# Fifteen small loads on ScalarE's queue, and a wait for them, behind the copy of wq's product

## The chip, the cores and the metric

The kernel runs on one core of a Trainium2 chip. The metric is the device time of one execution in microseconds (us). The chip's engines run side by side and synchronise by semaphores: TensorE (matrix products), VectorE, ScalarE and GpSimd (elementwise work), and SyncE (SP), which only issues transfers. Sixteen DMA engines move the data. SP's loads go through one queue of these (queue 1 in the profile), ScalarE's through another (queue 10).

## The reference

One decode step for two rows x of 1024 numbers: attention over a cache, and a small MLP mixer, mixed by a gate.

```python
# x (2,1,1024); caches (2, 4 heads, 32768, 128); wq (1024,4096); wo (4096,1024); w3 (1024,3584); w4 (3584,1024)
g = sigmoid((x * gate_w).sum(-1, keepdims=True))
q = (x @ wq) -> (2, 32 heads, 1, 128)          # 8 query heads share one head of the cache
p = softmax(q @ k^T * 128 ** -0.5)             # over 32768 positions
a = (p @ v) @ wo
x1 = x + hs                                     # hs: shifts along a sequence of length 1 leave zeros
b = x1 + gelu(layernorm(x1) @ w3) @ w4
out = g * a + (1 - g) * b
```

With a sequence of length 1 all four shifts give zeros, so w1 and w2 are not read. All is float32.

## The kernel before

**Tiles.** Everything large passes through a ring of two buffers, `load0` and `load1` (in the code `ring[j]` or `flat[j]`), of 128 rows by 64 KB each, 8.4 MB. One load fills one buffer: 128 rows, each one packet of up to 64 KB. wq comes in two loads, w3 in two (56 KB a row), each of the eight pairs of batch and head (a "head" below) in two of K and two of V, w4 in two in the middle, wo in three and four small ones into `tail` at the end.

**The order.** All of these loads are issued by SP, written out in order in `load` (L218): each waits for a mark that the buffer is free again, then issues. The marks that matter at the start: w3's two loads wait for wq's products of that buffer (`q0`, `q1`), K of head 0 for w3's products (`h0`, `h1`), V of head 0 in the first buffer for the first half of head 0's products with K (`k0`), in the second buffer for VectorE's word `k1_free`, when all of these products are done. ScalarE issues one load, xg (x and the gate's weights), at the very start (L244).

**The start of the program on the engines.** TensorE multiplies x with wq (`project`, L358) into two banks, sc0 and sc1. VectorE copies sc0 and ScalarE sc1 (L407, L409) into `row`. VectorE rearranges them (L415), TensorE turns them (L421), and VectorE writes the result as q (`q_pad`, `q_cur`). TensorE then multiplies the normalised x with w3 (L358 again) into sc2 and sc3, which VectorE and ScalarE copy (L444, L446); VectorE rearranges (L451), TensorE turns (L459), and VectorE and ScalarE compute the gelu (L463 to L475). Behind L459 TensorE enters the loop over heads (`turn`): products with K (L494), maxima, softmax, transposes (L511), products with V (L520). The loop runs four heads, the products with w4 (L373, 512 columns each), four heads and the products with wo that fit the ring.

A `Line` is an engine with its own semaphore: `mark` has an instruction add one to it, `after` makes the engine wait for marks or for a semaphore's count. A load adds 16 to its semaphore when it has landed.

Of the kernel before, what the change touches and what calls it, by code (L numbers as in the profile page):

```python
# [73 lines left out]
def kernel(  # L74
# [52 lines left out]
    nc = tc.nc  # L127
    scale = DH ** -0.5

    def new(name, *shape, parts=P):  # L130
        return nc.alloc_sbuf_tensor(name, [parts, *shape], F32).ap()

    def bank(name):
        return nc.alloc_psum_tensor(name, [P, 512], F32).ap()
# [45 lines left out]
    f = new("f", REP)  # L180
    so_far = new("so_far", D // 2)
    out_sb = new("out_sb", 2, CHUNK)

    sc = [bank(f"sc{i}") for i in range(NI)]
    tr = [bank(f"tr{i}") for i in range(2)]
# [8 lines left out]
    def sem(name):  # L194
        cleared.append(nc.alloc_semaphore(name))
        return cleared[-1]

    stored = nc.alloc_semaphore("stored")
    pe, dve, act, pool = (Line(e, sem(n)) for e, n in (
        (nc.tensor, "pe"), (nc.vector, "dve"), (nc.scalar, "act"), (nc.gpsimd, "pool")))  # L200
# [2 lines left out]
    landed = [sem(f"landed{i}") for i in range(2)]  # L203
    w_in = [*landed, sem("w_in2")]
    got_x = sem("got_x")
    issued = sem("issued")
    copied = sem("copied")
    middle = slice(BASE, BASE + 2 * ROWS)
# [198 lines left out]
    d_q = dve.mark(nc.vector.tensor_copy(row[:, 0], sc[0]))  # L407
    act.after(done)
    a_q = act.mark(nc.scalar.copy(row[:, 1], sc[1]))  # L409

    twice = p.rearrange("p i t w q -> p (i t w q)")[:, :REP * P * 2].rearrange(
        "p (h w i q) -> p h w i q", h=REP, w=PART, i=2)
# [34 lines left out]
    n = KF // G  # L447
# [234 lines left out]
```

## Time and profile before

| | |
|---|---|
| median of 2 runs | 773.11 us (773.02 to 773.20) |
| profiled execution | 773.22 us, span 771.7 us |
| transferred | 331.48 MB in 6647 packets, 430 GB/s over the span |
| busy: TensorE / VectorE / ScalarE | 437.2 / 94.4 / 60.7 us |
| TensorE's mean granted clock | 0.77 |

The span runs from the first to the last instruction. Times in the timeline are microseconds from its start: start, time taken, engine, line, operation, the tile written and the tiles read, sizes, count, and in brackets the idle time before it with what ended it. An engine's name with a q (SPq, ACTq) is its sequencer, which waits and issues transfers. A row of the DMA view is a queue with its packets, megabytes and the share of 16 engines' time that they took in the stretch asked for; issues are listed with the microseconds from issue to landing. A row of a table by stretches gives for each engine the busy time and count, then TensorE's granted clock, the DMA share and GB/s.

### The profile page before, as it was taken

To read this page: it belongs to the slowest core of one execution; us is meant where nothing else is said; L and a number is where in the kernel's file an instruction comes from. 1 tells how busy PE (TensorE), PEld (TensorE's weight loads), DVE (VectorE), ACT (ScalarE), POOL (GpSimd) and SP (SyncE) were. 2 spreads that over 40 slices of the span, in tenths; PEclk is the share of its full clock that TensorE was granted. 3 is DMA by queue.
4 is the path that set the end of the run, shared out by engine and by line. 5 is a ranking of instruction groups with operands and counts; after the bars stand their busy time and mean duration, and the time that the engine had idled before them with its cause. 6 is when DMAs were issued, how large, how long until landed. Compare 5 with 4: busy or idle time off the path is not lost. (4 is left out here: it accounts for less than half of the span.)

```text
span 771.7 us, 7007 instructions
## 1 busy us (share of the span) xinstructions
PE 437.2 (57%) x3116; PEld 191.4 (25%) x3116; DVE 94.4 (12%) x269; ACT 60.7 (8%) x144; POOL 4.4 (1%) x13
## 2 busy tenths in 40 slices
PE   0574747465656464546465456564645474556577
PEld 0231413232323232223221123231322232223232
DVE  1110202100210021002100002100210021002110
ACT  0000002000200020002100002000200020002000
POOL 2000000000000000000000000000000000000000
PEclk9977666866886778776876668767877777768769
DMA  9999999999999999999999999999999999999997
GB/s 381 435 436 436 435 436 435 436 432 435 435 435 435 435 428 435 428 435 435 427 437 437 432 435 435 435 435 435 435 435 435 435 435 431 435 435 435 421 427 321
DMA packets 6647, 331.48 MB, mean 430 GB/s; under 512 B 872, under 2 KB 1008, under 8 KB 1264
## 3 DMA queue, kind: packets, MB, share of 16 engines
q1 hardware_dynamic: 6496, 331.36, 99.4%
q8 instruction: 6, 0.10, 0.0%
q10 hardware_dynamic: 144, 0.01, 0.0%
q14 instruction: 1, 0.01, 0.0%
HBM read 331.36 MB, written 0.01 MB: 429 GB/s over the span
## 5 line engine op out<-in xcount | busy, mean ns | idle before, releaser
L494 PE MATMUL sc<-load,q_cur 128*32 128x512 f32 x1024 | 148.5, 740 | 128.9 <-PEq L53 128.9
L520 PE MATMUL pv<-load,pt 128*32 128x512 f32 x1024 | 135.7, 690 | 88.1 <-PEq L53 88.1
L494 PEld LDWEIGHTS sc<-load,q_cur 128*32 128x32 f32 x1024 | 53.7, 132 | 218.0 <-issue 213.2
L520 PEld LDWEIGHTS pv<-load,pt 128*32 128x32 f32 x1024 | 40.8, 125 | 173.0 <-issue 173.0
L511 PE MATMUL sc<-wide,p 128*128 128x128 f32 x256 | 43.7, 343 | 22.8 <-PEq L53 22.8
L577 DVE TENSOR_REDUCE mx<-sc 128x1 f32<-128x512 f32 x32 | 21.4, 689 | 286.9 <-PE sc L494 286.9
L561 ACT ACT_TABLE_LOAD x8 | 10.3, 1283 | 487.4 <-ACTq L53 487.4
L511 PEld LDWEIGHTS sc<-wide,p 128*128 128x128 f32 x256 | 39.5, 182 | 30.0 <-issue 30.0
L373 PE MATMUL acc<-load,w_pad 128*32 128x512 f32 x224 | 32.9, 730 | 18.9 <-PEq L53 18.9
L594 DVE COPY pt<-sc 64x256 f32<-64x256 f32 x64 | 25.9, 415 | 79.2 <-PE sc L511 78.4
L567 ACT COPY pt<-sc 64x256 f32<-64x256 f32 x64 | 23.5, 368 | 83.1 <-PE sc L511 80.6
L599 DVE COPY pv_sb<-pv 128x512 f32<-128x512 f32 x16 | 10.3, 687 | 147.9 <-PE tr L526 147.9
L530 PE MATMUL tr<-sel,pv_sb 128*128 128x8 f32 x128 | 19.7, 290 | 11.8 <-PEq L53 11.8
L530 PEld LDWEIGHTS tr<-sel,pv_sb 128*128 128x128 f32 x128 | 19.2, 237 | 12.3 <-issue 12.3
L358 PE MATMUL sc<-load,x_pad 128*32 128x512 f32 x128 | 18.0, 724 | 7.3 <-PEq L53 7.3
L561 ACT ACTIVATE p<-sc,bias 128x512 f32<-128x512 f32 x32 | 21.6, 686 | 0.1
L358 PE MATMUL sc<-load,xn_pad 128*32 128x384 f32 (+1 forms) x128 | 14.2, 600 | 10.3 <-PEq L53 10.3
L373 PEld LDWEIGHTS acc<-load,w_pad 128*32 128x32 f32 x224 | 9.1, 131 | 41.0 <-issue 41.0
L343 PE MATMUL tr<-xg_sb,perm 128*128 128x16 f32 x4 | 1.0, 372 | 23.0 <-DMA xg_sb<-xg 23.0
L590 DVE COPY p<-p 128x256 f32<-128x256 f32 x32 | 9.4, 294 | 26.7 <-ACT p L561 26.7
L358 PEld LDWEIGHTS sc<-load,xn_pad 128*32 128x32 f32 x128 | 4.5, 120 | 20.5 <-issue 20.5
L358 PEld LDWEIGHTS sc<-load,x_pad 128*32 128x32 f32 x128 | 4.7, 131 | 19.7 <-issue 19.7
(89 smaller groups left out, 91.9 us busy)
## 6 DMA issues: line engine op xcount, KB each, us to landing
load<-w SPq DMA_DIRECT2D x4, 7168.0 KB, 25.3
load<-wo SPq DMA_DIRECT2D x1, 7168.0 KB, 27.3
load<-wo SPq DMA_DIRECT2D x1, 4608.0 KB, 17.9
load<-wo SPq DMA_DIRECT2D x1, 2560.0 KB, 23.7
tail<-wo SPq DMA_DIRECT2D x1, 1024.0 KB, 25.7
tail<-wo SPq DMA_DIRECT2D x1, 640.0 KB, 26.8
load<-kt SPq DMA_DIRECT2D x16, 29.8
load<-vt SPq DMA_DIRECT2D x16, 29.2
```

What stands on the lines that cost most here:

```text
L358: last = nc.tensor.matmul(b[C * g:C * g + C, :hi - lo], pad[:, k], t[:, o + lo:o + hi], start=(k == 0), stop=(k == KD - 1))
L373: inst = nc.tensor.matmul(acc[lo:lo + C], lhsT, rows[:, g * (D // 2):(g + 1) * (D // 2)], start=False, stop=last, skip_group_check=True)
L494: last = nc.tensor.matmul(sc[i][C * g:C * g + C], q_cur[:, w, s], ring[j][:, w, o:o + 512], start=(s == 0 and w == 0), stop=(s == 1 and w ...
L511: last = nc.tensor.transpose(sc[k][:, t * P:(t + 1) * P], pair.rearrange("p w q -> p (w q)"), ident)
L520: last = nc.tensor.matmul(pv[C * g:C * g + C], pt[j][w][:, lo:lo + C], ring[j][:, w, o:o + G * DH], start=(j == 0 and w == 0 and t == 0), ...
L530: last = nc.tensor.matmul(tr[1][:, w * REP:(w + 1) * REP], pv_sb[:, s, w].rearrange("p i q -> p (i q)"), sel[:, s], start=(s == 0), stop=( ...
L561: nc.scalar.activation(p[:, i, :, :PART], sc[i].rearrange("p (t q w) -> p t w q", t=NT, w=PART), AF.Exp, bias=bias, scale=scale, accum_out ...
L567: nc.scalar.copy(*halves(1, j, c)).then_inc(pt_in, 1)
L577: last = [nc.vector.reduce_max(out=mx[:, k:k + 1], in_=sc[k], axis=AX.X) for k in ((1, 2) if i == 2 else (i,))][-1]
L590: nc.vector.tensor_copy(p[:, i, :, PART], p[:, i, :, 0]).then_inc(to_pe, 1)
L594: nc.vector.tensor_copy(*halves(0, j, c)).then_inc(pt_in, 1)
L599: last = nc.vector.tensor_copy(pv_sb[:, :, :, i], pv.rearrange("p (s q w) -> p s w q", q=HALF, w=PART))
```

## The change

ScalarE, when it has copied its half of wq's product, waits for that copy, issues fifteen loads, and waits until all have landed. The n-th load has n rows of 16 + n numbers from the beginning of head 0's K; they go to a tile of their own that nothing reads. Nothing else changes; line numbers behind the insertion rise by up to six.

```diff
     out_sb = new("out_sb", 2, CHUNK)
+    told_sb = new("told_sb", 15, 32, parts=16)
...
     got_x = sem("got_x")
+    told = sem("told")
...
     act.after(done)
     a_q = act.mark(nc.scalar.copy(row[:, 1], sc[1]))
+    act.after(a_q)
+    for n in range(1, 16):
+        nc.scalar.dma_start(told_sb[:n, n - 1, :16 + n], kt[0, 0, :n, :16 + n]).then_inc(told, 16)
+    act.after((told, 15 * 16))
```

## Prediction

> **What bounds the kernel now.** I read the head of the page first (busy shares, the transfer row), then its queues.
>
> ```profile
> PE 437.2 (57%) x3116; PEld 191.4 (25%) x3116; DVE 94.4 (12%) x269; ACT 60.7 (8%) x144; POOL 4.4 (1%) x13
> DMA  9999999999999999999999999999999999999997
> q1 hardware_dynamic: 6496, 331.36, 99.4%
> q10 hardware_dynamic: 144, 0.01, 0.0%
> ```
>
> TensorE is busy 57% of the span and ScalarE 8%; the 16 DMA engines are busy in every slice. Queue 1 (SP's transfers) fills 99.4% of them, queue 10 (ScalarE's one load, xg) next to nothing. So the kernel takes as long as its 331 MB take, plus every stretch in which queue 1 is empty. Work on ScalarE costs nothing until it delays the issue of a load past the moment at which queue 1 runs dry. The question is whether this change does that.
>
> The packet count gives the unit: xg's 128 rows made 144 packets, which is 128 rows and one telling (the write to its semaphore) on each of 16 engines.
>
> **The change in the program.** It touches ScalarE alone, behind its copy of half of wq's product. Before, ScalarE had there:
>
> ```order
> L333 ACTIVATE gate<-tr 128x2
> L409 COPY pt<-sc 128x512 [waits pe]
> L446 COPY pt<-sc 128x384 [waits pe]
> L468 ACTIVATE u<-u 128x112 [waits dve]
> L558 UNCONDITIONAL_BRANCH
> ```
>
> Now, from the twelfth of the fifteen loads on:
>
> ```order
> L414 DMA told_sb<-kt 12x28
> L414 DMA told_sb<-kt 13x29
> L414 DMA told_sb<-kt 14x30
> L414 DMA told_sb<-kt 15x31
> L452 COPY pt<-sc 128x384 [waits pe,told]
> L474 ACTIVATE u<-u 128x112 [waits dve]
> ```
>
> What moved: the copy of w3's product (L446, now L452) waited for TensorE alone and now waits also until all fifteen loads have landed. Line numbers below are those of before. Behind that copy stands a chain: VectorE rearranges both halves (L451), TensorE turns them (L459), only then come head 0's first products with K (L494), and their end lets SP issue the first V load (L218). In the timeline:
>
> ```profile
> 51.48 0.59 ACT L409 COPY pt<-sc 128x512 f32<-128x512 f32 x1 [23.33 <-PE sc L358]
> ...
> 85.17 0.48 ACT L446 COPY pt<-sc 128x384 f32<-128x384 f32 x1 [33.11 <-PE sc L358]
> 85.17 0.69 DVE L444 COPY pt<-sc 128x512 f32<-128x512 f32 x1 [26.27 <-PE sc L358]
> 85.89 2.08 DVE L451 COPY p<-pt 128x896 f32<-128x896 f32 x2
> 88.03 6.14 PE L459 MATMUL tr<-wide,p 128*128 128x8 f32 x28 [2.92 <-DVE p L451]
> ...
> 96.47 9.39 PE L494 MATMUL sc<-load,q_cur 128*32 128x512 f32 x64 [2.30 <-PEq L53]
> ...
> 105.92 20.32 SPq L218 DMA_DIRECT2D load<-vt  x2
> ```
>
> **When the small loads land.** The trace has one load of queue 10 beside queue 1's big ones: xg, at the start. Its issue, and the transfers of one stretch of 2.4 us and of the end:
>
> ```profile
> 0.74 0.39 ACTq L244 DMA_DIRECT2D xg_sb<-xg  x1
> xg_sb<-xg ACTq DMA_DIRECT2D x1, 12.0 KB, 22.1
> ```
>
> ```profile
> DMA packets 32, 1.05 MB, mean 438 GB/s; under 512 B 16, under 2 KB 16, under 8 KB 16
> q1 hardware_dynamic: 16, 1.05, 100.8%
> q10 hardware_dynamic: 16, 0.00, 0.5%
> ```
>
> The second fence is the DMA view from 4.5 to 6.9 us: 16 rows of 64 KB from queue 1 and 16 rows of 96 B from queue 10, one of each on every engine. So the engines take turns, one packet of each queue; a small packet costs nothing but waits out a whole 64 KB row. Nine packets of xg on each engine needed nine turns, hence 22.1 us for 12 KB.
>
> The trace also has one transfer of fewer than 16 rows, the output's 8, in the DMA view from 770 to 772 us:
>
> ```profile
> q1 hardware_dynamic: 16, 0.01, 1.8%
> ```
>
> Sixteen packets: 8 rows and 8 tellings, so a transfer of n rows below 16 uses n engines, one row each. If these are always the same first n, the fullest engine gets a row and a telling from each of the fifteen loads: 30 packets, and needs 30 turns. Nothing in this trace names the engines, so the bounds are 30 (always from the same end) and 15 (240 packets spread evenly over 16). I take 30: every load is split for itself, and to spread them one load would have to start where the last one ended, of which the trace has no sign. The Trainium skill, "DMA: Bandwidth & Descriptors", in the section on why a DMA increments its semaphore by 16 and not by 1, says that a load issued from SP or ScalarE takes the lowest-numbered engines, which would make it 30; the output's count agrees with that section on how many engines take part, and no run so far shows which.
>
> ScalarE starts to issue at 51.48 + 0.59 = 52.1 us. The way from issue to an engine's first packet is about 1 us (SP's first loads: issued at 0.74, the DMA view up to 1.7 us has none).
>
> ```profile
> 0.74 0.88 SPq L245 DMA_DIRECT2D load<-wq  x2
> ...
> DMA packets 0, 0.00 MB, mean 0 GB/s; under 512 B 0, under 2 KB 0, under 8 KB 0
> ```
>
> Fifteen issues at xg's 0.39 take to 58 us, two packets every 0.39 us for an engine that takes one in 2.1 to 2.4, so issuing is never the limit, even at several times that cost. The turns of queue 1 that then pass, in the DMA view from 53.3 to 113.6 us, and from 113.7 to 115.6:
>
> ```profile
> q1 hardware_dynamic: 464, 25.95, 99.5%
> ...
> q1 hardware_dynamic: 32, 1.05, 127.8%
> ```
>
> 464 / 16 = 29 turns per engine up to 113.6 us; the 30th comes with the second K load's telling, which 13 of the engines reach between 113.7 and 114.2:
>
> ```profile
> DMA packets 26, 0.85 MB, mean 1704 GB/s; under 512 B 13, under 2 KB 13, under 8 KB 13
> ```
>
> The other three come by 115.6. And at this point queue 1 runs dry in the changed kernel, since the next load waits for the chain above; whatever is still in queue 10 then passes at once. What remains is the time from a packet to its reader, seen at xg: its last 32 packets, between 21.7 and 22.5 us, and the instruction that waited for them.
>
> ```profile
> q10 hardware_dynamic: 32, 0.00, 2.6%
> ...
> 22.89 0.18 DVE L308 TENSOR_TENSOR xw<-xg_sb 128x16 f32<-128x16 f32 x1 [17.21 <-DMA xg_sb<-xg]
> ```
>
> Some half a microsecond. So the last small load lands at **about 114.3 us** (113.8 and 0.5), 115.7 if the fullest engine is one of the late three, hardly later however its packets are spread.
>
> **The sum.** From the landing: ScalarE's copy 0.1 + 0.48 + 0.07, VectorE's 2.14 (85.89 to 88.03), TensorE's turning 6.14, the 64 products 9.39 (both K loads lie there, so without the 2.30 of waiting), 0.06 to SP's issue: 18.4 us. SP issues the first V load at 132.7 where it did at 105.92. It lands on queues that stand empty, as xg's neighbour, the first wq load, did: 22.1 us. Before, it was queued behind K and took:
>
> ```profile
> load<-vt SPq DMA_DIRECT2D x1, 29.2
> ```
>
> 132.7 + 22.1 = 154.8 against 105.92 + 29.2 = 135.1: **19.7 us later**. Nothing gives it back: the DMA row is full from there to the end. Nothing is added either: TensorE goes straight on with head 0's other K products, so the second V load is issued near 143, before the first has landed, as before. The 240 small packets themselves cost the engines nothing measurable (queue 10 in the stretch above: 0.5%). The profiled execution took 773.22 us around a span of 771.7, the median is 773.11: 773.1 + 19.7 = 792.8, say **793 us**, 2.6% more. A measurement of this kernel tells about 2% from no change, so slower means above 788.6.
>
> Bounds of the terms: the late engine adds 1.4; head 0's second 64 products took 9.94, so 0.6 more is possible. Downwards the clock:
>
> ```profile
> 88.00:94.20 6.20, 6.14 (x28) 6.05 (x28) 0.00 (x0) 0.00 (x0) 0.00 (x0) 0.50 0.83 359
> 96.40:105.90 9.50, 9.39 (x64) 2.55 (x64) 1.18 (x5) 0.00 (x0) 0.00 (x0) 0.75 1.03 443
> 60.60:66.80 6.20, 6.18 (x68) 1.80 (x60) 0.00 (x0) 0.00 (x0) 0.00 (x0) 1.00 0.98 419
> ```
>
> The turning ran at a granted 0.50 and the 64 products at 0.75; at 1.00, 68 products took 6.18. A full clock in both would save 3.1 + 3.2, giving 786.6. TensorE will have stood idle for 32 us before (3 before), so I take the slow values.
>
> **The rivals.**
> - *The small loads are hidden.* Spread evenly, an engine has 15 packets, and the DMA view from 53.3 to 80 us (the row below) shows 231 / 16 = 14 turns of queue 1 already. They land by some 81 us, before 85.17, when the copy could start: no change, 773. A little later would still be free: the first V load may be issued until 112.7 (1 us before queue 1 runs dry at 113.8), so the copy may start until 112.7 - 18.4 = 94.3 us, some 22 turns. Only what comes behind that costs, microsecond for microsecond. The same holds if several packets of queue 10 pass in one turn, from two per turn on (15 turns again); xg's 16 and 16 speak against that. The Trainium skill, "DMA: Bandwidth & Descriptors", section on queues, rings and completion order, says an engine drains typically 9 to 17 descriptors of one queue before it switches. By that rule the time would be 773; the trace disagrees for xg, one per turn. Chance 0.11, of which 0.06 for spreading. This is the rival on the other side, and 94.3 us is the point from which it decides.
>
> ```profile
> q1 hardware_dynamic: 231, 11.73, 101.6%
> ```
>
> - *Queue 10 stops SP.* If SP's issue were held while ScalarE's packets wait, queue 1 would dry up after w3 at 75 to 76.5 us, the rest of queue 10 would pass at once, and K would start some 2 to 3 us late: 776. Against it: the two issue rows at 0.74 ran side by side. Chance 0.04.
> - *TensorE starts at full clock* after the long rest: 787 to 790. Chance 0.03.
>
> **How the numbers follow.** Forecast 0.82: 793, from 791 to 796 by its bounds. The range 786 to 798 holds it and the quick clock, about 0.84; the hidden case stays outside. Slower: 0.82 and part of the clock's, 0.83; same: 0.16; faster 0.01, as no term saves more than the three late engines' 1.4 us, which a pause lets catch up.
>
> **What would show it.** Queue 10: 144 + 240 = 384 packets. ScalarE's L452 starts near 114.4 instead of 85.17. In the transfer row there is a gap of some 19 us after 115 us (the seventh slice near 0), all later slices full. The first V issue near 132.7, and every later event some 20 us later. Wrong if L452 starts at 85 (spread or several per turn), or if a wait of SP before K's issue appears at 67 us.

## The result, and the profile after

The changed kernel takes 794.42 us (median of 2 runs, 793.94 to 794.91), the kernel before 773.11: a ratio of 1.0276, with an interval from 1.0231 to 1.032. The forecast was 793 in a range from 786 to 798.

The page of the changed kernel, the rows that answer to those of before (busy shares, the transfer row, the queues):

```profile
span 792.4 us, 7023 instructions
PE 434.2 (55%) x3116; PEld 188.7 (24%) x3116; DVE 94.4 (12%) x269; ACT 60.6 (8%) x144; POOL 4.4 (1%) x13
DMA  9999972999999999999999999999999999999997
q1 hardware_dynamic: 6496, 331.36, 96.9%
q10 hardware_dynamic: 384, 0.03, 0.0%
```

All busy times are within 1.5% of those before (TensorE 434.2 against 437.2 us, its weight loads 188.7 against 191.4). What is new is one hole in the transfer row: a 7 and a 2 in the sixth and seventh slices, everything behind them full. Queue 10 has 384 packets, 240 more. The rest of the story is in the timeline around the hole (line numbers are the changed kernel's: L452 is L446 of before, L465 is L459, L500 is L494, L220 is L218):

```profile
51.79 5.53 ACTq L414 DMA_DIRECT2D told_sb<-kt  x15
...
86.69 0.69 DVE L450 COPY pt<-sc 128x512 f32<-128x512 f32 x1 [27.64 <-PE sc L360]
114.91 0.48 ACT L452 COPY pt<-sc 128x384 f32<-128x384 f32 x1 [63.15 <-DMA told_sb<-kt]
115.49 2.08 DVE L457 COPY p<-pt 128x896 f32<-128x896 f32 x2 [28.11 <-ACT pt L452]
117.63 6.14 PE L465 MATMUL tr<-wide,p 128*128 128x8 f32 x28 [31.00 <-DVE p L457]
123.70 15.90 PE L500 MATMUL sc<-load,q_cur 128*32 128x512 f32 x128
...
132.80 7.25 SPq L220 DMA_DIRECT2D load<-vt  x2
```

The reader is to see the bracket of L452: ScalarE stood for 63.15 us and a small load ended it. VectorE's half of the same copy had started at 86.69. The chain behind it ran at its usual lengths, and SP issued the first V load at 132.80, not at 105.92. The DMA view of the stretch before that, from 115.9 to 133.5 us, has a single packet, an instruction fetch, and no load; the issue row is the first V load's:

```profile
DMA packets 1, 0.02 MB, mean 1 GB/s; under 512 B 0, under 2 KB 0, under 8 KB 0
q8 instruction: 1, 0.02, 0.4%
load<-vt SPq DMA_DIRECT2D x1, 22.3
```

So most of the loss is a stretch of some 18 us in which the transfers, on which the kernel's time hangs, stand still. Most engines stand still somewhat longer, since fourteen of the second K load's sixteen tellings have passed by 114.4 us (a view further down shows them).

### The profile page after: what moved, and what is told of

Same layout as the page of the kernel before. It is cut to its first block, busy times and chain, and to the rows that moved or that the text cites. A ratio compares the mean times of both kernels' runs of the same rounds, so it can differ in the third digit from the quotient of the medians.

```text
span 792.4 us, 7023 instructions
## 1 busy us (share of the span) xinstructions
PE 434.2 (55%) x3116; PEld 188.7 (24%) x3116; DVE 94.4 (12%) x269; ACT 60.6 (8%) x144; POOL 4.4 (1%) x13
## 5 line engine op out<-in xcount | busy, mean ns | idle before, releaser
L500 PE MATMUL sc<-load,q_cur 128*32 128x512 f32 x1024 | 145.7, 729 | 119.0 <-PEq L53 119.0
L500 PEld LDWEIGHTS sc<-load,q_cur 128*32 128x32 f32 x1024 | 52.5, 131 | 206.4 <-issue 200.0
L536 PE MATMUL tr<-sel,pv_sb 128*128 128x8 f32 x128 | 17.4, 271 | 11.8 <-PEq L53 11.8
L465 PE MATMUL tr<-wide,p 128*128 128x8 f32 x28 | 6.1, 362 | 31.0 <-DVE p L457 31.0
L360 PE MATMUL sc<-load,xn_pad 128*32 128x384 f32 (+1 forms) x128 | 16.1, 667 | 9.4 <-PEq L53 9.4
L536 PEld LDWEIGHTS tr<-sel,pv_sb 128*128 128x128 f32 x128 | 16.9, 212 | 12.3 <-issue 12.3
L465 PEld LDWEIGHTS tr<-wide,p 128*128 128x128 f32 x28 | 6.0, 332 | 31.7 <-DVE p L457 31.7
```

What stands on the lines that cost most here:

```text
L360: last = nc.tensor.matmul(b[C * g:C * g + C, :hi - lo], pad[:, k], t[:, o + lo:o + hi], start=(k == 0), stop=(k == KD - 1))
L465: last = nc.tensor.matmul(ht_ps[:, o:o + PAIRS], both[:, c, w].rearrange("p i q -> p (i q)"), compact, start=True, stop=True)
L500: last = nc.tensor.matmul(sc[i][C * g:C * g + C], q_cur[:, w, s], ring[j][:, w, o:o + 512], start=(s == 0 and w == 0), stop=(s == 1 and w ...
L536: last = nc.tensor.matmul(tr[1][:, w * REP:(w + 1) * REP], pv_sb[:, s, w].rearrange("p i q -> p (i q)"), sel[:, s], start=(s == 0), stop=( ...
```

## The experiments

The theory: a small packet waits out one packet of queue 1 on its engine; the fullest engine (15 rows and 15 tellings) sets when the wait ends; and the wait costs only what it makes the V load late beyond the moment at which queue 1 runs dry. The edits below are made to the changed kernel, unless it is said otherwise.

**The wait one instruction later.** ScalarE issues the same loads but waits for them behind its copy of w3's product.

```diff
         nc.scalar.dma_start(told_sb[:n, n - 1, :16 + n], kt[0, 0, :n, :16 + n]).then_inc(told, 16)
-    act.after((told, 15 * 16))
...
     a_h = act.mark(nc.scalar.copy(row[:, 1, :F // G - 512], sc[3][:, :F // G - 512]))
+    act.after((told, 15 * 16))
```

> The same fifteen loads, but ScalarE waits for them behind its copy of w3's product instead of ahead of it. Theory (the cost is the late copy, and through it the late V load): the copy starts near 86 us, queue 1 never runs dry, 773 us, although the last small load still lands near 114 us. Rival (the 240 packets slow the big transfers, or SP's issues): 790 us or more as in the changed kernel.

Measured: 773.41 us, ratio 1.0003 (0.9993 to 1.0013). In its timeline the copy (here L451) starts when TensorE lets it, and the wait stands before the gelu's tanh (L474), where nobody on the path to a load is behind it:

```profile
85.07 0.48 ACT L451 COPY pt<-sc 128x384 f32<-128x384 f32 x1 [33.31 <-PE sc L360]
...
105.89 20.20 SPq L220 DMA_DIRECT2D load<-vt  x2
...
114.73 0.30 ACT L474 ACTIVATE u<-u 128x112 f32<-128x112 f32 x1 [29.18 <-DMA told_sb<-kt]
```

The loads land just as late (114.73), the packets are the same, the V load is issued when it was before (105.89 against 105.92), and the time is that of before. The 240 packets cost nothing that the time shows; the place of the wait makes the loss.

**One row each.** Fifteen loads of one row.

```diff
-    for n in range(1, 16):
-        nc.scalar.dma_start(told_sb[:n, n - 1, :16 + n], kt[0, 0, :n, :16 + n]).then_inc(told, 16)
+    for n in range(15):
+        nc.scalar.dma_start(told_sb[:1, n, :17], kt[0, 0, :1, :17]).then_inc(told, 16)
```

> Fifteen loads of one row each instead of 1 to 15 rows: 30 packets in all instead of 240. Theory (every load starts on the same engine, and each packet there waits for one of queue 1): that engine still has 30 packets, the copy starts near 114.9 us, 794 us. Rival (loads are spread over the engines, or the number of packets in all decides): two or so packets an engine, landed by 62 us, 773 us.

Measured: 793.23 us, ratio 1.0261 (1.0244 to 1.0278). The page's row of queue 10 and the copy:

```profile
q10 hardware_dynamic: 174, 0.01, 0.0%
...
114.79 0.48 ACT L452 COPY pt<-sc 128x384 f32<-128x384 f32 x1 [61.90 <-DMA told_sb<-kt]
```

30 packets (174 less xg's 144) delay the copy as long as 240 did, so their number in all does not count. In the DMA view of this run from 80 to 104 us they pass at the pace of one engine's rows: 11 of them, beside 170 / 16 = 10.6 packets of queue 1 on each engine.

```profile
q1 hardware_dynamic: 170, 10.09, 97.3%
q10 hardware_dynamic: 11, 0.00, 0.0%
```

Two explanations fit these times: all fifteen loads use the same engine, or the loads pass one after another, each a row and a telling long, wherever they go. The changed kernel's DMA view from 56 to 60 us decides between them:

```profile
q1 hardware_dynamic: 46, 1.72, 99.7%
q10 hardware_dynamic: 21, 0.00, 0.4%
```

That is the time of about two rows on an engine. If the loads went one after another, at most the first two could have passed, 6 packets; there are 21. The single transfers in that trace carry their sizes, and load n's rows have 64 + 4n bytes: at the steady pace of one engine a row of 68, 72, 76, 80 bytes and so on passes at 56.20, 58.36, 62.60 and 66.84 us, up to 120 at 109.28 and 124 at 114.14, a row of every load in order; other rows of the fifteenth load pass from 62.51 us on. So the loads run side by side, and one engine has a row and a telling of each. This settles the choice between 30 turns and 15 that the trace of before left open; which of the sixteen engines it is, the trace does not say.

**Eight loads of 16 rows.** More packets, but evenly on all engines.

```diff
-    for n in range(1, 16):
-        nc.scalar.dma_start(told_sb[:n, n - 1, :16 + n], kt[0, 0, :n, :16 + n]).then_inc(told, 16)
-    act.after((told, 15 * 16))
+    for n in range(8):
+        nc.scalar.dma_start(told_sb[:16, n, :31], kt[0, 0, :16, :31]).then_inc(told, 16)
+    act.after((told, 8 * 16))
```

> Eight loads of 16 rows: 256 packets in all, more than in the changed kernel, but 16 on every engine. Theory: 16 turns from 56 us on end near 84.8 us, landed by 85.4, hidden: 773 us, the copy at most half a microsecond late. Rival (packets in all decide): 794 us or more.

Measured: 773.59 us, ratio 1.0006 (0.9996 to 1.0015). The copy waited 0.9 us past VectorE's, a little longer than expected, and this cost nothing:

```profile
q10 hardware_dynamic: 400, 0.03, 0.0%
...
86.72 0.69 DVE L450 COPY pt<-sc 128x512 f32<-128x512 f32 x1 [27.81 <-PE sc L360]
87.62 0.48 ACT L452 COPY pt<-sc 128x384 f32<-128x384 f32 x1 [36.03 <-DMA told_sb<-kt]
```

256 small packets are hidden where 30 on one engine are not. The total decides nothing. What is small here is the number of loads: with up to 16 rows a load costs the fullest engine a row and a telling, so eight loads make 16 turns. Fifteen loads of 16 rows were not run; by the theory they would make 30 turns on every engine and be paid for like the change.

**Thirteen and nine loads.** Two points between none and fifteen: the loads of 1 to 13 rows, and those of 1 to 9 (the edit is in the brackets of the loop and the count waited for; shown for thirteen).

```diff
-    for n in range(1, 16):
+    for n in range(1, 14):
...
-    act.after((told, 15 * 16))
+    act.after((told, 13 * 16))
```

> The loads of 1 to 13 rows only. Theory: 26 turns on the fullest engine; with 21 turns past at the end of the first K load (94.4 us) the 26th comes at 106.6 us, the copy starts near 107.2 us instead of 114.9, SP issues V near 125.5, and the time is 786 us. Rival (the wait ends only when queue 1 runs dry, however many packets are left): copy at 114.9, 794 us.

> The loads of 1 to 9 rows only. Theory: 18 turns, the last near 89.6 us, the copy starts near 90.2 us, 5 us later than before, and this is free since up to 94.3 us nothing is lost: 773 us. Rival (each microsecond that the copy is late is paid): 778 us.

Measured: thirteen 787.83 us, ratio 1.0182 (1.0164 to 1.02); nine 773.14 us, ratio 1.0 (0.9991 to 1.001). The copy and the first V load with thirteen:

```profile
109.69 0.48 ACT L452 COPY pt<-sc 128x384 f32<-128x384 f32 x1 [57.52 <-DMA told_sb<-kt]
...
127.31 7.25 SPq L220 DMA_DIRECT2D load<-vt  x2
```

and with nine:

```profile
90.23 0.48 ACT L452 COPY pt<-sc 128x384 f32<-128x384 f32 x1 [38.94 <-DMA told_sb<-kt]
...
108.20 17.43 SPq L220 DMA_DIRECT2D load<-vt  x2
```

With nine the copy is 5 us later than before (90.23 against 85.17), the V load 2.3 us later (before, TensorE stood 2.30 us waiting for the first K load, which takes up the rest), and the time is the same: V is still issued ahead of the 112.7 us that the prediction gives as the last free moment. With thirteen the wait ends 5.2 us earlier than with fifteen and V is issued 5.5 us earlier: it does not end at a fixed moment, but with the last packet's turn. The expectation there was one turn too early (copy at 107.2, 786 us; it came 2.5 us later, and so did the time, by 1.8): in that run the first load's packet gets its turn later than I had counted, see below.

**Thirty loads of one row.** Twice the turns that queue 1 offers before it runs dry.

```diff
-    told_sb = new("told_sb", 15, 32, parts=16)
+    told_sb = new("told_sb", 30, 32, parts=16)
...
-    for n in range(1, 16):
-        nc.scalar.dma_start(told_sb[:n, n - 1, :16 + n], kt[0, 0, :n, :16 + n]).then_inc(told, 16)
-    act.after((told, 15 * 16))
+    for n in range(30):
+        nc.scalar.dma_start(told_sb[:1, n, :17], kt[0, 0, :1, :17]).then_inc(told, 16)
+    act.after((told, 30 * 16))
```

> Thirty loads of one row: 60 packets on one engine, twice the changed kernel's. Theory (a small packet waits for a packet of queue 1 and costs nothing by itself): the 30 left when queue 1 runs dry at 113.8 us pass within a microsecond or two, the copy starts near 115 to 117 us, 794 to 796 us. Rival (a small packet takes its 2 us by itself, whatever queue 1 does): the copy near 56 + 60 x 2 = 176 us, 855 us.

Measured: 795.97 us, ratio 1.0299 (1.0282 to 1.0316). The DMA view from 113.8 to 114.4 us, and the copy:

```profile
q10 hardware_dynamic: 32, 0.00, 3.5%
q1 hardware_dynamic: 11, 0.00, 1.0%
...
117.14 0.48 ACT L452 COPY pt<-sc 128x384 f32<-128x384 f32 x1 [64.83 <-DMA told_sb<-kt]
```

32 packets of queue 10, more than half of the 60, pass within 0.6 us as soon as queue 1 has nothing left; for the other 28 it took from 52 to 114 us. The waiting is for queue 1's rows, not for anything that a small packet does itself. The copy still starts 2.35 us later than with fifteen one-row loads (114.79). This time does not go into the packets: between 114.2 and 117.1 us there is none of queue 10 in the DMA view. It goes by before their tellings arrive: the trace's updates of the semaphore that ScalarE waits for come one every 0.18 us, the last sixteen from 114.45 to 117.12.

**Half the row.** The changed kernel with every load of the ring as two transfers of half the columns (`halved`, left out here, cuts a tile and its source in two); the fifteen loads and the wait stay ahead of the copy. The same edit on the kernel before is the control.

```diff
     def load(dst, src, sem, *marks):
         sp.after(*marks)
-        nc.sync.dma_start(dst, src).then_inc(sem, 16)
+        for d, s in halved(dst, src) if sem in w_in else [(dst, src)]:
+            nc.sync.dma_start(d, s).then_inc(sem, 16)
...
-            pe.take(landed[T], 16)
+            pe.take(landed[T], 32)     # likewise the other waits for the ring; wq's first loads are halved too
```

> The changed kernel, its fifteen loads and the wait as they are, but every load of the ring goes as two transfers of half the columns, so that a packet of queue 1 is 32 or 28 KB instead of 64 or 56. Theory (a small packet waits for one packet of queue 1): a turn takes 1.06 to 1.21 us; from 56 us on 30 turns end near 84 us, the copy starts between 85 and 88 us, queue 1 does not run dry, and the time is that of the kernel before, 773 us, give or take 2 for the added tellings and issues. Rival (the small loads wait for whole loads, or for queue 1 to run dry): the copy near 115 us, 794 us.

> The kernel before with every load of the ring as two transfers of half the columns, as a control for the run with half rows. Theory: twice the packets of the same bytes cost nothing that can be told, 773 to 775 us. Rival (a packet has a cost of its own of a tenth of a microsecond or more): 5900 more packets on 16 engines, 370 each, would give 40 us or more.

Measured: with the small loads 776.33 us, ratio 1.0041 (1.0026 to 1.0056); the control 776.27, ratio 1.0041 (1.0026 to 1.0056). On the page and in the timeline of the first:

```profile
q1 hardware_dynamic: 12400, 331.36, 99.5%
q10 hardware_dynamic: 384, 0.03, 0.0%
...
86.85 0.69 DVE L456 COPY pt<-sc 128x512 f32<-128x512 f32 x1 [27.84 <-PE sc L366]
86.91 0.48 ACT L458 COPY pt<-sc 128x384 f32<-128x384 f32 x1 [35.06 <-PE sc L366]
```

The bracket of the copy now names TensorE again. The same 384 packets of queue 10, the same wait in the same place, but turns of half the length: the small loads land before the copy could start, and the two kernels with half rows are equal. The length of queue 1's rows is what a small packet pays. The halving itself costs 3 us in both (776.27 against 773.27 for the kernel before, run beside it), against 0 to 2 expected: put to the 5904 more packets, 369 on each engine, that is 8 ns each.

No kernel beat the one before; the variants that equal it take the wait off the path or keep it short.

## Why the prediction was right

- *The turns.* One packet of queue 10 for each packet of queue 1 held: the copy started at 114.91 us where 114.4 was said, the last two packets passing in the same stretch as the second K load's tellings (DMA view of the changed kernel from 113.6 to 114.4 us):

```profile
q1 hardware_dynamic: 14, 0.00, 1.0%
q10 hardware_dynamic: 2, 0.00, 0.2%
```

  The Trainium skill, "DMA: Bandwidth & Descriptors", section on queues, rings and completion order, has an engine drain typically 9 to 17 descriptors of a queue before it switches. The runs disagree, if a packet of the profile is a descriptor: in the one-row run 11 small packets pass beside 10.6 of queue 1 on an engine from 80 to 104 us, one and one. The prediction's 773 us by that rule is too quick: it lets queue 10 alone pass several packets in a turn. If queue 1 too held an engine for 9 to 17 rows, the two queues would share the turns as one and one do, and the loads need not be hidden.
- *The way to the first turn was too short.* I gave a small packet 1 us from issue to its first turn, taken from a start with empty queues. The changed kernel issued at 51.79 and has no packet of queue 10 up to 56 us; the first four come between 56.0 and 56.4:

```profile
q10 hardware_dynamic: 4, 0.00, 0.8%
```

  That is 4.2 us at the least. In this run it cost nothing, which is luck: the sum counted only packets of queue 1 that began behind 53.3 us, and the first small packet passed just as the first of these rows ended (56.20). So the 30 turns came as counted, the last two at 114.14 and 114.16. With thirteen loads the first load's row passed only at 58.13, one row of queue 1 later, and this is the 2.5 us by which the expectation failed. With fifteen one-row loads it passed at 58.25, and that was hidden: three packets instead of two were left when queue 1 ran dry. That an engine had taken more than one row of queue 1 ahead would explain the late start; no run tells this apart from a slower issue.
- *The spread.* 30 packets on one engine: shown by the one-row loads (793.23), together with the changed kernel's transfers, in which the loads run side by side. The Trainium skill, "DMA: Bandwidth & Descriptors", in the section on why a DMA increments its semaphore by 16 and not by 1, has a load of few rows take the lowest-numbered engines; the runs agree in that it is always the same one, and do not show its number.
- *The chain.* From the copy's start to V's issue 17.9 us (114.91 to 132.80), where 18.3 was said; TensorE did turn at the slow clock (granted 0.50 from 117.6 to 123.8 us) and took 6.14, as said. V's load took 22.3 on empty queues, 22.1 was said. It landed at 132.80 + 22.3 = 155.1, against 135.1 before: 20.0 us later, 19.7 was said. The 0.5 us of the late copy and the 0.4 us of the shorter chain nearly cancel.
- *Nothing given back, nothing added.* Nearly: the output's transfer is issued at 791.07 instead of 770.34, 20.7 us later. The 0.7 us more come at the second V load: issued at 139.73 it landed 35.5 us later, at 175.2; before, issued at 125.91, it took 28.5 and landed at 154.4. That is 20.8 us later, and the difference then stays to the end. Why the second V load came that much further behind the first is open. The profiled executions differ by 20.7 us (793.94 against 773.22), the medians by 21.3.

```profile
load<-vt SPq DMA_DIRECT2D x1, 35.5
load<-vt SPq DMA_DIRECT2D x1, 28.5
```

- *The rivals.* The hidden case is real, but it needs fewer turns than this change has, or shorter ones: nine loads, eight loads, or half rows. Its point of decision held: a copy at 90.23 was free, one at 109.69 was paid for. SP was not held: it issued the first K load at 68.23, while queue 10 was full, right behind w3's first products, which ended at 68.16 (66.86 before, with these products earlier), and with the wait moved the V load was not late at all (105.89).

```profile
61.10 7.06 PE L360 MATMUL sc<-load,xn_pad 128*32 128x512 f32 x64
68.23 18.78 SPq L220 DMA_DIRECT2D load<-kt  x2
```


## What to carry to other kernels

A small load beside a queue of large ones takes as many turns as the fullest engine has packets of it, most of them as long as one row of the large loads; here 30 turns, 26 behind a row of 2.1 us (56 KB) or 2.4 us (64 KB) and four behind a telling. Issue it ahead of need, gather small rows into few loads (thirty rows in as many loads wait longer than 128 rows in eight), and put the wait for it where no issue of a large load hangs on what follows. In a kernel bound by its transfers, price any wait by the moment at which the queue would run dry: up to there it is free, and beyond it is paid in full.

## What was not expected of the hardware

- On an engine that is free, the packets of small loads pass at once (32 between 113.9 and 114.2 us with thirty loads), but their tellings arrive 0.18 us apart, so that sixteen loads left over made the copy 2.35 us later than two did with fifteen loads. I had taken it for nothing.
- Fewer than 16 rows make the issue no dearer: fifteen issues took 5.53 us, 0.37 each, against 0.39 for xg's 128 rows. The fifteen one-row loads took 4.86 us, 0.32 each, the eight of 16 rows 3.65 us, 0.46 each.
- A packet of queue 1 costs some 8 ns beside its bytes, if the 3 us of the half rows are put to packets alone.
